# One more slot of P turned by DMA in the odd pairs, and the order of all steps taken from a table

## The chip, the cores and the metric

The kernel runs on one core of one Trainium2 chip. The time is the device time of one execution in microseconds (us). Before the change it is 818.27 us, the median of 3 runs (817.58 to 820.57).

## What is computed

The inputs are q, k and v with 8 batches, 12 heads, 448 rows and 64 columns, all float32. The reference, cut to what matters:

```python
q_n, k_n = rmsnorm(q, g_q), rmsnorm(k, g_k)
scores = q_n @ k_n.T / sqrt(64)
attn = exp(scores - max(scores));  attn = attn / (sum(attn) + 1e-9)
x = (attn @ v)                     # heads side by side: (8, 448, 768)
h = maximum(x @ w_in, 0.0)         # w_in: 768 x 1024
conv = sum(conv_w[i] * shifted(h, i - 1) for i in range(3))   # along the 448 rows
out = (h * sigmoid(conv)) @ w_out  # w_out: 1024 x 768
```

## The kernel before, in words

**The work and its tiles.** The 96 heads are taken two at a time: 48 pairs, n = 0 to 47, six to a batch. A pair's two 448 x 448 score matrices are cut into seven slots, each with 128 rows of P and 448 columns. For each pair the kernel loads q, k and v, squares and sums (`square`, `square_sum`, L384, L395), makes the reciprocal root in nine small steps (`rsqrt`, L416 to L431), applies it (`apply_rms`, the helper's L121, into the tile sq) and turns k and q (`qk_transpose`, L455). `v_bound` (L542) takes the largest v. `scores` (L633) puts two slots at a time into PSUM, `soft_max` takes the largest of a row on DVE, and `soft_exp` (L647) writes the exponentials of a slot to a tile e on ACT.

**Two ways for P.** The product with v (`pv`, L764) needs P turned, in the tile PT. From pair ten on the matrices go through TensorE as pairs of float16 numbers, a high and a low part, with three products for one. There a slot of P takes one of two ways:

- through TensorE: `p_transpose` (L677) turns the float32 exponentials in four blocks, `p_evac` (helper L109, ACT or DVE) copies them out of PSUM as the high part, and `p_low` (L693, DVE) subtracts to get the low part;
- through the DMA: `p_hi` (helper L109) writes the high part into one of four buffers ph, `p_lo` (helper L121) the low part, and `p_turn` (L669) issues a transposing DMA from the queue SP straight into PT.

`nd(n)` says how many slots go by DMA: none below pair ten, six of seven in even pairs, five in odd ones. Pairs below ten use float32 on TensorE and turn all seven slots there.

**The two products after it.** `x_scale`, `x_hi` and `x_lo` make x of a pair; `in_part` (L849) is three matmuls of the product with w_in, `in_relu` to `in_lo` make the gated h on ACT, DVE and POOL, and `out_part` (L918) is four or eight matmuls of the product with w_out. Matmuls of one batch are spread between the attention of the next one. At the start the two weights are loaded and split into float16 parts (`convert`, L228 to L236, `bound`, L286, `split`, `rest`, L313).

**What sets the order.** All of this is 4908 steps. A planner inside the kernel gives each step a due time (`PACE`, `SHIFT`, `base`), lists what it needs (`needs`) and which engines can take it at what cost (`options`), and then places step after step, always the one that its model could start first, weighed with the due time. The order so made is the order in which each engine, and the queue SP, runs its instructions; it fixes too which of two or three engines takes a step, and which PSUM bank. An engine never passes a waiting instruction.

Of the kernel before, what the change touches and what calls it, by code (L numbers as in the profile page):

```python
# [19 lines left out]
PH = dict(  # L20
    sh=10, sm=15, sw=0.0, f_pl=0.0375, f_ql=0.2981, f_lo=0.1439, f_rms=0.7618, f_sq=0.4266,
    T=17.3833, ti=41.4349, si=4.1104, so=8.3395, hop=0.86442, beta=0.01242, wi0=-50.4678,
    wi1=121.7101, wo0=25.8448, wo1=191.2771, cw=148.8611, p_evac=0.4491, p_hi=1.3981, p_lo=0.4268,
    p_rms=0.5211, p_v=0.5458, p_x=0.0, p_g=4.2741, p_relu=21.8931, p_cv=3.9149, p_ev=23.6856,
    sp=0.0518, nbulk=4, p_rs=0.0491, p_sq=1.6068, p_w=6.9093, v0=26.5245, nd=6, ng=5, cs=5, ct=3,
    cm=9, ne=5, n2=0, n1=10, q1=10, nf=10, pvs=4, p_sa=2.9086, p_c0=0.4899, p_ca=0.4662,
    p_ss=3.937, p_qh=2.0393, p_ql=2.1586, p_ph=3799.4719, p_pl=2744.2083, f_ca=0.232, f_cv=0.0,
    f_ev=0.0, f_evac=0.0, f_g=0.0, f_relu=0.0114, f_v=0.1905, f_w=0.0633, f_pl_early=0.0372,
    f_ql_early=0.301, f_lo_early=0.3185, f_rms_early=0.0046, f_sq_early=0.0131,
    p_evac_early=0.258, p_hi_early=0.2963, p_lo_early=0.4289, p_rms_early=0.4454,  # L30
    p_v_early=0.3813, p_x_early=0.7905, p_g_early=0.9472, p_relu_early=12.3484,
    p_cv_early=10.9077, p_ev_early=22.3546, p_rs_early=0.0395, p_sq_early=17.492,
    p_w_early=182.8497, p_sa_early=4.9153, p_c0_early=0.4104, p_ca_early=16.3838,
    p_ss_early=3.937, p_qh_early=3.8564, p_ql_early=3.3133, p_ph_early=10.4483,
    p_pl_early=23.3405, f_ca_early=0.5227, f_cv_early=0.2129, f_ev_early=0.0247, f_evac_early=0.0,
    f_g_early=0.0, f_relu_early=0.2356, f_v_early=0.0161, f_w_early=0.0241, early=9, f_sa=0.4067,
    f_sa_early=0.1734, f_x_early=0.0301, f_hi=0.1205, f_hi_early=0.0, f_x=0.0463, f_c0=0.0028,
    f_rs=0.0, f_rs_early=0.0121,
)
PACE = [  # L40
    19.5944, 19.8948, 16.4648, 19.6082, 13.2431, 14.9147, 11.825, 10.1937, 22.5592, 19.3385,
    25.6034, 15.2494,
]
SHIFT = dict(
    prepare=1144.827, load_g=408.072, make_g=1103.747, load_cw=607.34, make_cw=-40.693,
    load=31.489, convert=814.375, bound=1163.815, bound_max=1185.545, bound_turn=683.508,
    scale=1588.906, in_factor=1190.579, split=219.334, rest=-3.777, out_factor=13.562,
    load_k=276.969, load_q=-23.205, square=644.465, square_sum=176.751, rsqrt=204.636,
    apply_rms=466.723, qk_transpose=49.891, qk_hi=700.581, v_load=1413.524, v_bound=41.813,
    scores=154.339, soft_max=-4.033, soft_exp=1280.605, p_transpose=1204.209, p_evac=1.285,  # L50
    sum_add=984.669, sum_step=662.828, sum_store=217.691, sum_load=507.067, pv=524.491,
    x_scale=111.36, x_hi=969.665, x_lo=4.428, v_max=-17.121, v_turn=12.147, v_scale=833.202,
    qk_lo=-6.58, q_hi=-16.441, q_lo=262.726, q_turn=-4.581, p_hi=807.409, p_lo=-4.961,
    p_turn=606.498, p_low=0.411, v_hi=539.567, v_lo=817.516, moe_scales=2733.662,
    in_part=1631.107, in_relu=283.451, in_conv=494.692, in_tanh=706.753, in_gate=507.891,
    in_hi=1047.689, in_lo=2.125, in_carry=156.421, out_scales=760.141, out_part=104.873,
    out_evac=1.046, out_store=35.83, sum_spread=1.673, sum_turn=2.156,
)
SCHED = {}
ON_ACT = ""  # L60
# [20 lines left out]
def tile_attention_moe(ctx: ExitStack, tc, q, k, v, g_q, g_k, w_in, conv_w, w_out, out):  # L81
# [7 lines left out]
    P = 128  # L89
# [7 lines left out]
    T = PH["T"]  # L97

    def base(n):

        return sum(PACE[:n]) + max(n - len(PACE), 0) * T

    def queue(kind):
        return nc.scalar if kind in ON_ACT.split() else nc.sync

# [65 lines left out]
    def at(t, fn, *args):  # L171
        plan.append((t + SHIFT.get(fn.__name__, 0.0), len(plan), fn, args))
# [77 lines left out]
    def plan_weight(name, w, w32, s_col, free, t0, t1, after):  # L250
# [105 lines left out]
    def load_k(n):  # L356
        x = new("qkf", n, [PB, 2, 2, NB, D], F32)
        rows = slice(n * 2 * S, (n + 1) * 2 * S)
        queue("lk").dma_start(x[:, 1], heads(kf[rows].rearrange("(h p t) d -> p h t d", h=2, t=NB), n))

    def load_q(n):
# [147 lines left out]
    def plan_qk(n):  # L509
        s = base(n)  # L510
        at(s - 45.0, load_k, n)
        at(s - 45.0, load_q, n)
        for i in sides(n):
            at(s - 24.0, square, n, i)
            at(s - 22.0, square_sum, n, i)
            if duo(n)[0] == n:
                for j in range(NRS):
                    at(s - 20.0 + 0.3 * j, rsqrt, n, j, i)
        for i in (1, 0):
            at(s - 15.0 - i, apply_rms, n, i)  # L520
            if i == 0 and n >= PH["q1"]:
                at(s - 13.0, q_hi, n)
                at(s - 12.0, q_lo, n)
                at(s - 11.0, q_turn, n)
                continue
            at(s - 10.0 - i, qk_transpose, n, i)
            at(s - 8.0 - i, qk_hi, n, i)
            if not whole(n):
                at(s - 6.0 - i, qk_lo, n, i)


    def v_load(n):
        t = new("v", n, [PB, 2, NB, D], F32)
        rows = slice(n * 2 * S, (n + 1) * 2 * S)
        queue("lv").dma_start(t, vf[rows].rearrange("(h p t) d -> p h t d", h=2, t=NB))
# [24 lines left out]
    def plan_v(n):  # L560
        b, i = divmod(n, NP)
        t = base(max(n - 7, 0)) + PH["v0"] + 3.0 * min(n, 7)
        at(t, v_load, n)
        at(t + 20.0, v_bound, n)
        if i == NP - 1:
            at(t + 20.5, v_max, b)
            at(t + 20.6, v_turn, b)
            at(t + 22.0, v_scale, b)
# [31 lines left out]
    def nd(n):  # L600
        return 0 if n < PH["n1"] else (PH["nd"], PH["ne"], PH["nd"], PH["ng"])[n % 4]
# [108 lines left out]
    def sum_store(n):  # L710
        d = new("rd", n, [32, P], F32, pD)
        queue("rd").dma_start(d.rearrange("s (b i) -> b s i", b=4), old("rT", n))

    def shuffled(n):

        return n >= PH["sh"] and PH["sm"] >> n % 4 & 1
# [5 lines left out]
    def sum_load(n, h):  # L722
        d = old("rd", n)[:NS].rearrange("t p -> (t p)").rearrange("(h s) -> h s", h=2)
        if shuffled(n):
            r = fixed("row", n, rows).rearrange("(x p) s -> x p s", p=32)[:, 0]
            queue("rb").dma_start(r, d.unsqueeze(1).to_broadcast([2, 2, S]))
# [3 lines left out]
        queue("rb").dma_start(old("rB", n)[HALF[h]], d[h : h + 1].to_broadcast([64, S]))  # L730
# [59 lines left out]
    def plan_attention(n):  # L790
        s, d = base(n), (base(n + 1) - base(n)) / NS
        for g in groups(n):
            at(s + max(2 * g - n % 2, 0) * d, scores, n, g)
        for j in range(NS):
            at(s + j * d + 1.0, soft_max, n, j)
            at(s + j * d + 2.0, soft_exp, n, j)
            if j < nd(n):
                at(s + j * d + 3.0, p_hi, n, j)
                at(s + j * d + 4.0, p_lo, n, j)
                at(s + j * d + 5.0, p_turn, n, j)  # L800
                continue
            at(s + j * d + 4.0, p_transpose, n, j)
            at(s + j * d + 5.0, p_evac, n, j)
            if nd(n):
                at(s + j * d + 6.0, p_low, n, j)
        s += NS * d
        at(s + 2.0, sum_add, n)
        at(s + 2.5, sum_step, n)
        at(s + 3.0, sum_turn, n)
        at(s + 4.0, sum_store, n)  # L810
        for h in range(loads(n)):
            at(s + 6.0, sum_load, n, h)
        if shuffled(n):
            at(s + 7.0, sum_spread, n)
        if nd(n):
            at(s - 4.0, v_hi, n)
            at(s - 3.0, v_lo, n)
        for i, k in enumerate(pvs(n)):
            at(s + 8.0 + i, pv, n, k)
        at(s + 13.0, x_scale, n)  # L820
        at(s + 14.0, x_hi, n)
        at(s + 15.0, x_lo, n)
# [107 lines left out]
    def out_store(b, ch, half):  # L930
        row0 = out_place(b, ch)[1]
        queue("out").dma_start(
# [691 lines left out]
```

## Time and profile before

| what | before |
|---|---|
| median of 3 runs | 818.27 us |
| profiled execution, first to last instruction | 818.1 us |
| TensorE (PE) busy | 787.5 us, 96% |
| VectorE (DVE) busy | 704.5 us, 86% |
| ScalarE (ACT) busy | 683.4 us, 84% |
| GpSimd (POOL) busy | 445.9 us, 55% |
| DMA, share of 16 engines | 74.4% |

The profiled execution's span of 818.1 us is its own time here; no other time is given for it, and it lies 0.2 us below the median. Busy is the time in which at least one instruction of the engine runs. PE means matmuls, PEld loads of weights, SP the queue from which all DMAs are issued. A name like e_(25_5_5245 is the tile e of pair 25, slot place 5.

### The profile page before, as it was taken

To read this page: it belongs to the slowest core of one execution; us is meant where nothing else is said; L and a number is where in the kernel's file an instruction comes from. 1 tells how busy PE (TensorE), PEld (TensorE's weight loads), DVE (VectorE), ACT (ScalarE), POOL (GpSimd) and SP (SyncE) were. 2 spreads that over 40 slices of the span, in tenths; PEclk is the share of its full clock that TensorE was granted. 3 is DMA by queue.
4 is the path that set the end of the run, shared out by engine and by line. 5 is a ranking of instruction groups with operands and counts; after the bars stand their busy time and mean duration, and the time that the engine had idled before them with its cause. 6 is when DMAs were issued, how large, how long until landed. Compare 5 with 4: busy or idle time off the path is not lost.

```text
span 818.1 us, 16993 instructions
## 1 busy us (share of the span) xinstructions
PE 787.5 (96%) x5582; PEld 429.3 (52%) x5582; DVE 704.5 (86%) x1478; ACT 683.4 (84%) x1584; POOL 445.9 (55%) x575
## 2 busy tenths in 40 slices
PE   3889999999999999999999999999999999999998
PEld 1444555555555555555555565555555555555554
DVE  7999999999899989999899989999899988882420
ACT  4989999998899877998899887988899888981531
POOL 2222134585677656687578556686578566552220
PEclk9998999999999999999999999999999999999999
DMA  8765753369988999779998999889988997444001
GB/s 238 210 194 147 185 161 80 81 134 168 181 159 149 179 184 188 166 147 185 173 168 167 181 177 182 159 143 186 183 177 159 184 176 167 94 90 102 10 20 59
DMA packets 325453, 124.65 MB, mean 152 GB/s; under 512 B 270172, under 2 KB 321780, under 8 KB 325364
## 3 DMA queue, kind: packets, MB, share of 16 engines
q1 hardware_dynamic: 325364, 123.56, 74.4%
q8 instruction: 44, 0.72, 0.4%
q14 instruction: 45, 0.37, 0.2%
HBM read 48.20 MB, written 11.80 MB: 73 GB/s over the span
## 4 chain that ended last, share of the span: by engine, by line
PE 48%; DVE 13%; ACT 11%; DMA 6%; issue 4%; POOL 2%; SPq 2%; ACTq 0%; POOLq 0%; DVEq 0%
PE bank L918 21%; PE bank L849 11%; PE bank L764 6%; PE bank L633 6%; DMA PT<-ph 4%; PE bank L677 2%; ACT ph L109 2%; SPq L669 1%; PE bank L455 1%; POOL ph L121 1%; DMA rd<-rT 1%; DVE st L395 1%; DMA row<-rd 1%; DVE PT L693 1%; ACT bank L857 1%
## 5 line engine op out<-in xcount | busy, mean ns | idle before, releaser
L849 PE MATMUL bank<-x,wi 128*128 128x448 f16 x1152 | 231.7, 353 | 0.3 <-DVE PT L109 0.3
L918 PE MATMUL bank<-wo,gring 128*128 128x384 f16 (+1 forms) x1056 | 199.5, 327 | 1.0 <-ACT e_(34_4_7306 L647 0.8
L849 PEld LDWEIGHTS <-wi 128*128 128x128 f16 x1152 | 110.5, 98 | 103.9 <-issue 11.6
L918 PEld LDWEIGHTS <-gring 128*128 128x128 f16 (+1 forms) x1056 | 101.7, 99 | 67.9 <-issue 16.4
L633 PE MATMUL bank<-kT,qT 64*128 64x448 f16 (+3 forms) x1072 | 131.4, 392 | 1.3 <-ACT e_(3_2_713 L647 0.6
L764 PE MATMUL bank<-PT,vp 112*64 112x448 f16 x912 | 93.9, 354 | 1.4 <-ACT e_(27_0_5495 L647 1.0
L764 PEld LDWEIGHTS <-vp 112*64 112x64 f16 x912 | 50.5, 110 | 42.1 <-issue 15.0
L395 DVE TENSOR_REDUCE st<-sq 112x16 f32<-112x1024 f32 (+1 forms) x50 | 58.3, 1170 | 9.6 <-ACT sq L384 9.4
L633 PEld LDWEIGHTS <-qT 64*128 64x128 f16 (+1 forms) x912 | 33.2, 97 | 51.3 <-issue 31.6
L384 ACT ACTIVATE sq<-qkf 112x1024 f32<-112x1024 f32 (+1 forms) x48 | 49.6, 1033 | 5.2 <-DMA qkf<-in_q_dram 3.9
L121 POOL TENSOR_TENSOR sq<-qkf,st 112x512 f32<-112x512 f32 x38 | 39.9, 1056 | 19.1 <-issue 9.6
L121 POOL TENSOR_TENSOR x<-x,x 128x448 f16<-128x448 f32 x33 | 34.2, 1036 | 27.6 <-DVE x L109 12.3
L455 PE MATMUL bank<-ident,sq 112*128 112x112 f32 x232 | 33.0, 268 | 15.8 <-DVE G L974 10.3
L918 PE MATMUL bank<-wo,wi 128*128 128x384 f16 (+1 forms) x192 | 46.9, 326 | 0.0
L121 DVE TENSOR_TENSOR sq<-qkf,st 112x512 f32<-112x512 f32 x58 | 44.8, 791 | 0.1
L693 DVE TENSOR_TENSOR PT<-bank,PT 112x512 f16<-112x512 f32 x57 | 39.0, 684 | 3.2 <-ACT PT L109 2.8
L857 ACT ACTIVATE bank<-bank 128x448 f32<-128x448 f32 x64 | 34.4, 538 | 8.7 <-PE bank L849 7.9
L121 POOL TENSOR_TENSOR qkf<-sq,qkf 112x512 f16<-112x512 f32 x32 | 37.1, 1160 | 5.6 <-DVE sq L121 4.1
L455 PEld LDWEIGHTS bank<-ident,sq 112*128 112x128 f32 x232 | 25.8, 144 | 26.3 <-issue 14.6
L109 ACT COPY PT<-bank 112x512 f32<-112x512 f32 x62 | 36.2, 605 | 2.6 <-PE bank L677 2.3
L918 PE MATMUL bank<-wo,carry 128*64 128x384 f16 x192 | 34.0, 328 | 0.5 <-DVE c_(1_6_3169 L879 0.5
L542 DVE TENSOR_REDUCE vacc<-v 112x1 f32<-112x512 f32 x48 | 32.2, 674 | 2.4 <-DMA v<-in_v_dram 1.9
(2224 smaller groups left out, 1953.9 us busy)
## 6 DMA issues: line engine op xcount, KB each, us to landing
qkf<-in_k_dram SPq DMA_DIRECT2D x48, 224.0 KB
v<-in_v_dram SPq DMA_DIRECT2D x48, 224.0 KB
wo<-in_moe_w_in_dram SPq DMA_DIRECT2D x12, 512.0 KB
gring<-in_moe_w_out_dram SPq DMA_DIRECT2D x16, 384.0 KB
qkf<-in_q_dram SPq DMA_DIRECT2D x24, 224.0 KB
qkf<-in_q_dram SPq DMA_DIRECT2D x48, 112.0 KB
PT<-ph SPq DMA_TRANSPOSE x209
rB<-rd SPq DMA_DIRECT2D x20, 112.0 KB
```

The costliest lines, as they stand in the source:

```text
L109: (nc.scalar.copy if e == "ACT" else elementwise(e).tensor_copy)(dst, src)
L121: elementwise(e).tensor_tensor(dst, a, b, op=op)
L384: nc.scalar.activation(sq, x, AF.Square)
L395: nc.vector.tensor_reduce(st, sq, axis=AX.X, op=ALU.add)
L455: nc.tensor.transpose(ps[:, t * PB : (t + 1) * PB], x[:, t], ident[:PB, :PB])
L542: nc.vector.tensor_reduce(old("vacc", b)[:PB, i : i + 1], old("v", n).rearrange("p h t d -> p (h t d)"), axis=AX.X, op=ALU.max, apply_abso ...
L633: nc.tensor.matmul(ps[u][o, :S], lhs, rhs, start=(i == 0), stop=(whole(m) or i == 2),)
L693: nc.vector.tensor_tensor(turned(n, j, 1), held["t", ("p", n, j)][:PB].rearrange("p (k q) -> p k q", k=NB), turned(n, j, 0), op=ALU.subtract,)
L764: nc.tensor.matmul(ps[HALF[h], :S], lhs, rhs, start=(i == 0 and k == 0), stop=(i == pvs(n)[-1] and k == NB - 1),)
L849: nc.tensor.matmul(ps[:, :S], wi[:, wl, c, fc * P : (fc + 1) * P], old("x", b * NP + c)[:, xl], start=(i == 0), stop=(i == 3 * NP - 1),)
L857: nc.scalar.activation(ps, ps, AF.Relu, scale=2.0 ** -24)
L918: nc.tensor.matmul(ps[p0 : p0 + m, :NO2], g, wo[:, wl, fc, half * NO2 : (half + 1) * NO2], start=(i == 0), stop=(i == 3 * NFC - 1),)
```

## The change

`nd` becomes the list `ND`, with none for the first ten pairs and six for all others. So in the 19 odd pairs 11, 13, ... 47 slot place 5 leaves TensorE and goes by DMA: 19 `p_transpose`, 19 `p_evac` and 19 `p_low` go, 19 `p_hi`, `p_lo` and `p_turn` come. The planner with its due times and costs goes too. In its place stands a table of 4908 entries with the step, its engine and its PSUM banks; the steps are run in the table's order.

```diff
-    sp=0.0518, nbulk=4, p_rs=0.0491, p_sq=1.6068, p_w=6.9093, v0=26.5245, nd=6, ng=5, cs=5, ct=3,
-    cm=9, ne=5, n2=0, n1=10, q1=10, nf=10, pvs=4, p_sa=2.9086, p_c0=0.4899, p_ca=0.4662,
...
+ORDER = (
+    "$%&!!!#!$($!$)#!$*%!!*&!$+#!!.#!$&&!$q&!!+&!$,#!$-#!$.#!!/#!$3$!$s$!$/#!$0%!!#&!$r&!!,&!%a&!$4#!"
...
+ND = [0] * 10 + [6] * 38
...
     def nd(n):
-        return 0 if n < PH["n1"] else (PH["nd"], PH["ne"], PH["nd"], PH["ng"])[n % 4]
+        return ND[n] if 0 <= n < NPAIR else 0
...
-    while len(order) < len(steps):
-        best, free_banks = None, room()
...
+    for i in range(len(plan)):
+        a, b, e, z = (DIGITS.index(x) for x in ORDER[4 * i : 4 * i + 4])
+        fn, args = plan[len(DIGITS) * a + b]
+        step, e = (fn.__name__, *args), ("PE", "DVE", "ACT", "POOL", "SP")[e]
+        order.append((step, fn))
         on[step] = e
...
+        placed[step] = [y - 1 for y in divmod(z, 9) if y]
```

Nearly every step stands elsewhere than before. Steps that change engine, over the whole program: `apply_rms` from DVE to POOL (58 on DVE before, 12 now), `p_hi` (all 209 on ACT before; of 228 now 167 on ACT, 44 on POOL, 17 on DVE), `p_lo` (all 209 on POOL before; now 180, and 48 on DVE), `in_hi` (64 on ACT before; now 41, 17 on POOL, 6 on DVE), `in_lo` (64 on POOL before; now 50, 14 on DVE), `out_evac` (56 on ACT before; now 41, 15 on DVE), `p_evac` (33 on DVE before; now 9).

TensorE in pair 25, before: its slot place 5 is turned between two matmuls of the product with w_in (wi) and the scores of pair 26 (kT, qT).

```order
L849 LDWEIGHTS wi_84
L849 MATMUL bank_71<-x_4678,wi_84 128x448
L677 MATMUL bank_68<-ident,e_(25_5_5245 112x128 x4
L633 LDWEIGHTS qT_5058
L633 MATMUL bank_67<-kT_5070,qT_5058 128x448
```

The same place now: L1004 is `in_part`, L834 `p_transpose`.

```order
L1004 LDWEIGHTS wi_84
L1004 MATMUL bank_72<-x_4970,wi_84 128x448
L834 MATMUL bank_69<-ident,e_(25_6_5250 112x128 x4
L1004 LDWEIGHTS wi_84
L1004 MATMUL bank_73<-x_4755,wi_84 128x448
```

Place 5 is gone from TensorE; place 6 alone is turned there, between matmuls of the product with w_in.

ACT at the same pair, before: after the exponentials of places 5 and 6 it copies place 5 out of PSUM (PT from a bank).

```order
L647 ACTIVATE e_(25_5_5245,rsum_82<-bank_67,sst_(25_5_5232 128x448
L647 ACTIVATE e_(25_6_5262,rsum_82<-bank_66,sst_(25_6_5247 128x448
L109 CAST PT_5171<-bank_68 112x4x128
L109 CAST ph_79<-e_(25_3_5179 128x4x112
L109 CAST ph_80<-e_(25_4_5191 128x4x112
L109 CAST PT_5171<-bank_66 112x4x128
```

ACT now: L804 is `soft_exp`, L270 the copying helper.

```order
L804 ACTIVATE e_(25_6_5250,rsum_82<-bank_69,sst_(25_6_5226 128x448
L270 CAST ph_78<-e_(25_3_5182 128x4x112
L270 CAST ph_79<-e_(25_4_5199 128x4x112
L270 CAST ph_80<-e_(25_5_5216 128x4x112
L804 ACTIVATE e_(26_0_5271,rsum_81<-bank_67,sst_(26_0_5258 128x448
```

The copy of place 5 out of PSUM has become a third write into a buffer ph, behind which a low part and a DMA follow.

DVE at the start of the program, before, in pair 1's softmax: it applies the root to q of pair 2 (sq from qkf) between the largest v (vacc) of two pairs and a copy of P.

```order
L416 SCALAR_TENSOR_TENSOR st_228<-st_228 112x32
L542 TENSOR_REDUCE vacc_288<-v_291 112x1
L109 COPY PT_386<-bank_68 112x4x128
L121 TENSOR_TENSOR sq_229<-qkf_165,st_228 112x2x4x64
L639 TENSOR_REDUCE sst_(1_5_420<-bank_72 128x1
L542 TENSOR_REDUCE vacc_288<-v_332 112x1
```

POOL now, at that place: L282 is the helper of `apply_rms`, L577 to L590 are steps of `rsqrt`.

```order
L590 TENSOR_TENSOR st_254<-st_254 112x32
L588 TENSOR_TENSOR st_254<-st_254 112x32
L577 TENSOR_SCALAR st_254<-st_254 112x32
L578 TENSOR_TENSOR st_254<-st_254 112x32
L282 TENSOR_TENSOR sq_255<-qkf_138,st_254 112x2x4x64 x2
L857 TENSOR_SCALAR rsum_82<-rsum_82 128x7
```

Both applications of pair 2, q and k, stand on POOL now; one of them stood on DVE.

## Rows read from the trace of the kernel before

**Rows 1.** The page's first part: busy time and share of each engine.

```profile
PE 787.5 (96%) x5582; PEld 429.3 (52%) x5582; DVE 704.5 (86%) x1478; ACT 683.4 (84%) x1584; POOL 445.9 (55%) x575
```

**Rows 2.** By stretch: length; busy PE, PEld, DVE, ACT, POOL; granted clock; DMA; GB/s.

```profile
0.00:117.00 117.00, 96.19 (x543) 52.11 (x543) 109.45 (x264) 101.58 (x243) 32.18 (x72) 0.97 0.69 188
60.00:80.00 20.00, 17.91 (x87) 10.17 (x88) 19.81 (x48) 18.85 (x42) 5.04 (x12) 0.83 0.49 134
117.00:186.50 69.50, 68.26 (x420) 35.79 (x419) 66.72 (x142) 66.81 (x154) 39.51 (x45) 1.00 0.47 109
186.50:818.10 631.60, 623.03 (x4623) 341.38 (x4622) 528.37 (x1073) 515.05 (x1190) 374.22 (x459) 1.00 0.79 151
```

**Rows 3.** Engines that PE waited for, late and early: us in total, times, longest.

```profile
PE bank L455 <- DVE G L974: 10.3, 1, 10.3
...
PE bank L677 <- ACT e_(25_5_5245 L647: 0.7, 1, 0.7
...
PE bank L677 <- ACT e_(37_5_7912 L647: 0.4, 1, 0.4
PE bank L764 <- DMA PT<-ph: 0.4, 1, 0.4
```

**Rows 4.** The chain that ended last, pieces on PE: start us, us, what, matmuls.

```profile
275.00 0.44 PE bank L677 x4
...
277.33 0.76 PE bank L918 x4
...
278.53 1.30 PE bank L918 x8
...
755.57 27.24 PE bank L849 x144
```

**Rows 5.** Writers of ph and PT by tile: duration ns least/median/most, first and last start.

```profile
L669 SPq DMA_TRANSPOSE PT<-ph x209: 1231/1262/2733, 159.9 to 744.1; - x105
...
L121 POOL TENSOR_TENSOR ph<-e_(10_1_1782,ph x1: 1047/1047/1047, 158.2 to 158.2; 128x448 f16<-128x448 f32 x1
```

**Rows 6.** DVE, groups by line and shape: busy us, mean ns of one, idle before.

```profile
L121 DVE TENSOR_TENSOR sq<-qkf,st 112x512 f32<-112x512 f32 x58 | 44.8, 791 | 0.1
...
L542 DVE TENSOR_REDUCE vacc<-v 112x1 f32<-112x512 f32 x48 | 32.2, 674 | 2.4 <-DMA v<-in_v_dram 1.9
...
L313 DVE SCALAR_TENSOR_TENSOR wi<-wi,wsc 128x1024 f16<-128x1024 f32 x6 | 7.6, 1274 | 0.0
...
L109 DVE COPY PT<-bank 112x512 f32<-112x512 f32 x8 | 5.4, 679 | 0.9 <-ACT e_(8_1_1383 L647 0.5 <-PE bank L677 0.3
...
L424 DVE TENSOR_SCALAR st<-st 112x32 int32<-112x32 int32 x23 | 3.9, 170 | 0.2
L700 DVE TENSOR_SCALAR rsum<-rsum 128x7 f32<-128x7 f32 x12 | 3.6, 299 | 0.0
```

**Rows 7.** ACT, groups by line and shape, the same columns.

```profile
L109 ACT COPY PT<-bank 112x512 f32<-112x512 f32 x62 | 36.2, 605 | 2.6 <-PE bank L677 2.3
...
L109 ACT CAST x<-x 128x448 f16<-128x448 f32 x31 | 17.8, 574 | 6.1 <-DVE x L775 5.6 <-DVE x L778 0.4
...
L286 ACT ACTIVATE wo<-wo 128x384 f16<-128x384 f32 x16 | 8.8, 549 | 0.2
```

**Rows 8.** Time line of the end: the last store, issued from SP.

```profile
815.16 0.33 SPq L932 DMA_DIRECT2D out_dram<-c_('o'_7_3_1_10763  x1
```

**Rows 9.** DVE instructions with two inputs in SBUF: ns least/median/most.

```profile
L121 DVE TENSOR_TENSOR sq<-qkf,st x58: 636/682/1531, 9.5 to 685.8; 112x512 f32<-112x512 f32 x58
...
L121 DVE TENSOR_TENSOR x<-x,x x15: 582/615/985, 138.0 to 727.1; 128x448 f16<-128x448 f32 x15
```

**Rows 10.** Time line around P times v of pair 18, SP and PE.

```profile
301.40 2.73 SPq L669 DMA_TRANSPOSE PT<-ph  x2
...
307.37 2.43 PE L764 MATMUL bank<-PT,vp 112*64 112x448 f16 x23 [0.37 <-DMA PT<-ph]
```

**Rows 11.** ACT's wait for a free buffer ph: us in total, times, longest.

```profile
ACT ph L109 <- DMA PT<-ph: 26.4, 34, 2.6
```

More of the change, by code (lines that the diff above doesn't have):

```diff
@@ L40 @@
[L40 to L58, printed above, removed]
@@ L931, in out_store @@
         row0 = out_place(b, ch)[1]
[L932 removed]
+        nc.sync.dma_start(
             outf[row0 : row0 + P, half * NO2 : (half + 1) * NO2],
@@ L1357, in tile_attention_moe @@
-    PATIENCE = dict(
-        qk_hi="hi", q_hi="qh", q_lo="ql", apply_rms="rms", x_hi="x", x_lo="lo", in_hi="g", in_lo="g",
-        out_evac="ev", sum_add="sa", v_hi="hi", v_lo="lo", p_hi="ph", p_lo="pl", v_bound="v", rest="w", rsqrt="rs", square="sq", convert="c0", in_relu="relu", in_conv="cv", p_evac="evac", in_carry="ca",
-    )
-    def takes(name, *a):
-        if name in ("qk_transpose", "p_transpose", "bound_turn", "v_turn"):
-            return "t", (give(name, *a),)
-        if name in ("in_part", "out_part") and not a[-2] or name == "pv" and not a[-1]:
-            return "m", (give(name, *a),)
-        if name == "scores":
-            return "s", tuple(("soft_exp", *x) for x in members(*a))
-        if name == "in_conv" and not a[-1] or name == "out_evac":
-            return "c", (give(name, *a),)
-        return None
@@ L1387, in tile_attention_moe @@
-    steps = {(fn.__name__, *args): (t, i, fn) for t, i, fn, args in plan}
-    assert len(steps) == len(plan)
-    after, left, ready, done = {}, {}, {}, {}
-    for step in steps:
-        pre = {p for p in needs(*step) if p in steps}
-        left[step], ready[step] = len(pre), []
-        for p in pre:
-            after.setdefault(p, []).append(step)
-    waiting = {e: {} for e in ("PE", "DVE", "ACT", "POOL", "SP")}
-    MOE = ("in_", "out_", "moe_")
-    def patience(i, name, *a):
-        kind = ("p_" if i else "f_") + PATIENCE.get(name, "")
-        if a and isinstance(a[0], int) and a[0] < (1 if name.startswith(MOE) else PH["early"]):
-            kind += "_early"
-        return kind
@@ L1406, in enqueue @@
-    def enqueue(step):
-        for i, (e, c, dma) in enumerate(options(*step)):
-            t = max((end + lat["DMA" if dma else e] for end, lat in ready[step]), default=0.0)
-            waiting[e][step] = t + PH.get(patience(i, *step), 0.0), c, dma
-    sys.setrecursionlimit(20000)
-    due = {}
-    def urgency(step):
-        if step not in due:
-            due[step] = min(
-                [steps[step][0]] + [urgency(p) - PH["hop"] for p in after.get(step, ())]
-            )
-        return due[step]
@@ L1433, in tile_attention_moe @@
-    WINDOW = 4096 / 1200
-    free = dict.fromkeys(waiting, 0.0)
-    pmode, port = None, dict(DVE=0.0, POOL=0.0)
-    turn, held_by = None, {}
-    def mode(name, *a):
-        if name == "scores" and a[0] % 2 and not a[1]:
-            return "middle"
-        return name if name in ("pv", "scores") else ""
-    ringq = {"m": [], "c": [], "t": [], "s": []}
-    most = dict(s=PH["cs"], t=PH["ct"], m=PH["cm"], c=BUFS["c"])
-    last_in, placed = [None] * NBANK, {}
-    def back_at(step, e, dma):
-        if step is None:
-            return 0.0
-        if step not in done:
-            return None
-        x = engine[step]
-        return done[step] + LAT["DMA" if x[2] else x[0]]["DMA" if dma else e]
@@ L1574, in tile_attention_moe @@
-    SCHED.update(held_by=held_by, after=after, t=max(done.values()), t0=0.0, done=done, engine=engine, order=order)
+    order, placed, held_by, turn = [], {}, {}, None
+    for i in range(len(plan)):
[3 more added lines that the diff above has]
+        order.append((step, fn))
+        on[step] = e
+        placed[step] = [y - 1 for y in divmod(z, 9) if y]
+        if shared(e, step[0]):
+            if e == "DVE":
+                turn = step
+            elif turn:
+                held_by[step], turn = turn, None
@@ L1582, in tile_attention_moe @@
     with tc.manual_schedule():
-        for step in order:
-            taken[:] = placed.get(step, ())
+        for step, fn in order:
+            taken[:] = placed[step]
             start = len(nc.cur_bb.bb.instructions)
-            steps[step][2](*step[1:])
+            fn(*step[1:])
             if step in owners:
```

867 lines of the change are left out of this document (295 added, 572 removed).

## The prediction

> **What bounds the kernel now.** I read the busy shares first: matmuls run in 96% of the span, VectorE in 86%, ScalarE in 84%, GpSimd in 55% [rows 1]. Such shares are averages, so the second view is the busy time by stretch [rows 2]. It shows two regimes. From 117 us on, TensorE is busy in 68.3 of 69.5 us and then in 623.0 of 631.6 us: it alone sets the end there, and a microsecond less of matmul work is a microsecond less of span, as long as the others keep up. Before 117 us it is busy for 96.2 us only, while VectorE has 109.5 and ScalarE 101.6: there TensorE waits for what these two make. Third, the waits of TensorE [rows 3]: one of 10.3 us at the start, and after it nothing long; a turned P that came by DMA was waited for once, 0.4 us. Fourth, the pieces of the chain that lie on TensorE [rows 4], for the price of its work: 144 matmuls of the product with w_in take 27.24 us, 0.19 us each; eight of the product with w_out take 1.30 us, but four that stand alone after scores take 0.76 instead of 0.65, so a change between kinds of work costs about 0.11 us.
>
> **The parts, and what each costs.**
>
> *19 transposes leave TensorE.* Four blocks of one slot take 0.44 us [rows 4]; 19 x 0.44 = 8.3 us. From pair eleven on TensorE is the bound [rows 2], so all of it counts: -8.3. The Trainium skill speaks against this move (VectorE: DVE Perf Modes, The three transpose paths, and the rules behind it): it wants a 128 x 128 block turned on TensorE where PSUM will do, 390 ns against 1309 ns by DMA. If the longer way were paid by who waits, 19 x 0.92 us would be added, 17.5 us, and the time would be 836 us (an estimate from that page). The trace agrees that the DMA way is longer, 1262 ns for the issue alone [rows 5], but not that TensorE pays it [rows 3].
>
> *Waits in front of those transposes.* Two of them stand among the waits: 0.7 us for the exponential of pair 25 and 0.4 us for pair 37 [rows 3]. The instruction that waited is gone; the matmuls behind it don't need that slot. -1.1; it is 0 if the neighbour that now comes first waits as long.
>
> *Copies and low parts.* On VectorE and ScalarE 19 `p_evac` and 19 `p_low` go, and 19 `p_hi` and `p_lo` come; from 186.5 us on VectorE is busy 528 and ScalarE 515 of 632 us [rows 2], so either sign is hidden. Its cover is gone only if one of them comes near the whole stretch. GpSimd has 374 of 632 us there; it gives up 48 `p_lo` to VectorE and 14 `in_lo`, at 1.05 us each [rows 5], and takes 46 `apply_rms`, 44 `p_hi` and 17 `in_hi`. That leaves it some 50 us fuller by my count, still under 70%.
>
> *19 DMA transposes more.* Each holds SP for 1.26 us [rows 5], 24 us over 600. The 209 of before were waited for 0.4 us by TensorE [rows 3]. I take 0; the bounds are 0 and rival C.
>
> *The start.* By the order, the steps placed before the first scores of pair 8 (117 us in the trace) change so. VectorE loses three `apply_rms` (44.8/58 = 0.77 us), two `v_bound` (0.67), two `p_evac` (0.68), one `rest` (1.27) and seven small instructions at 0.17, and takes five `sum_add` of 0.30 [rows 6]: -2.3 - 1.3 - 1.4 - 1.3 - 1.2 + 1.5 = -6.0 us. ScalarE loses three `x_hi` at 0.57 and two `bound` at 0.55 and takes one `p_evac` at 0.58 (36.2/62) [rows 7]: -2.2 us. Both were close to full, so that point should come between 2.2 and 6.0 us earlier; I take the middle, 4.1. TensorE meanwhile has three `in_part` more (3 x 3 x 0.19 = 1.7 us) and two transposes of four blocks fewer (2 x 0.44), so 0.8 us of its later work is already done. Together -4.9; the bounds are 0 (the wait moves to a place I have not counted, the 10.3 us at the start stay in any case) and -6.8.
>
> *Changes of kind.* I counted in both orders how often TensorE goes from scores, P times v or the rest to another of the three: 264 before, 273 now. 9 x 0.11 = +1.0 us; the bounds are 0 and twice that.
>
> *The clock.* In the stretch from 60 to 80 us the granted clock is 0.83 on average [rows 2], so TensorE was at the lower of its levels (1.2 of 2.4 GHz) for a third of it; 0.17 x 20 = 3.4 us of full-speed time. It had been waiting on and off before. The new order keeps a start of the same kind, so I leave the dip: 0, with bounds of -3.4 (gone) and +3.4 (a second one).
>
> *The rest of the order.* Nearly every step has moved. From 117 us on TensorE is idle for 1.2 + 8.6 = 9.8 us [rows 2]; of that the last store, issued at 815.2 us, and the copy before it take some 4 us after the last matmul [rows 8], which stay, and 1.1 are counted. What is left, about 4.7, may go or double: 0, bounds -4.7 and +4.7.
>
> **Sum.** Against the profiled execution's 818.1 us: -8.3 - 1.1 - 4.9 + 1.0 = -13.3, that is 804.8. The median of the runs is 0.2 above the span of the profile, so **805 us**.
>
> **Rivals.**
>
> *A: the order gains more.* The start comes to its far bound (-1.9 more), the dip of the clock goes (-3.4) and the later idle time too (-4.7): 795. For it: the wait behind each of these is named above. Against it: three things must go well at once.
>
> *B: VectorE and GpSimd block each other.* Two inputs from SBUF make an instruction on VectorE run late beside GpSimd: `apply_rms` has a median of 682 ns but a longest of 1531, `x_lo` 615 and 985 [rows 9]. By the Trainium skill (SBUF — State Buffer, Who interferes with whom) such a pair excludes each other for a whole instruction; the rows agree for their slowest, whose excess of 0.85 us is no more than one GpSimd instruction of 1.05. 48 `p_lo` and 14 `in_lo` of this kind come to VectorE and 46 `apply_rms` leave it. If each of the 62 stood for half a GpSimd instruction, 0.52 us, VectorE would have 32 us more. It has 103 us free after 186.5 us [rows 2], most of it in the last 80; if a third of the 32 us falls where a matmul waits, 11 us are lost: **816**, no change. Against it: the mean of `apply_rms` lies only 0.09 us over its median (0.77 and 0.68), and that makes 62 x 0.09 = 5.6.
>
> *C: the turned P comes late, slower than before.* The way over TensorE from the exponential to a ready slot is 0.44 + 0.60 + 0.68, 1.7 us (the low part priced as the copy of the same shape) [rows 4, 6, 7]. By DMA it is about 0.57 for the high part, 1.05 for the low one, 1.26 for the issue [rows 5, 7], and then until the data is there: for pair 18 the second issue ended at 304.13 and P times v went on at 307.37 [rows 10], 3.2 us. That is 6.1, 4.4 longer. Now 61 of the high parts are written by GpSimd or VectorE, and they wait for a free buffer ph as ScalarE did, 34 times for 26.4 us [rows 11]; GpSimd's low parts, behind them in its queue, would hold up the next DMA. If P times v of each odd pair came 1.5 us late, 19 x 1.5 = 28.5 us would turn 805 into **833**. It decides where the cover runs out. Counted in TensorE's order with the prices above, between the scores of place 5 and P times v of an odd pair lie 12.4 us of matmuls at least and 18 in the middle; even pairs, which sent that place by DMA before, had 17.1 at least. So only the tight ones (three of 19 are under 14 us) are near it, and the chain of 6.1 us would have to double. Nearly no wait for it in the trace [rows 3] speaks against it too.
>
> *D: the change does less.* Transposes fall away, but the start stays as it is: 818.1 - 8.3 - 1.1 + 1.0 + 0.2 = 810. If the waits in the middle then double too, 815.
>
> **The numbers.** A measurement of this kernel can tell a change of about 0.5%, 4.1 us, from none; faster means under 814.2, slower over 822.4. Chances: the forecast, 799 to 810, 0.58; A, below 799, 0.14; D within the gain, 810 to 814, 0.10; B and the end of D, no change, 0.10; C, slower, 0.08. So faster 0.82, same 0.10, slower 0.08. The range has to leave out no more than 0.2: I cut A's far end at 796 and reach to B's lower part at 815, which leaves out about 0.05 below and 0.15 above.
>
> **What would show it.** Matmuls busy for about 776 us in a span of 805; 108 groups of `p_transpose` in place of 127; 228 DMA transposes into PT; the first scores of pair 8 at 113 us, with VectorE and ScalarE still near full before. The wait of P times v for its DMA stays under 2 us in all. Wrong would be: `pv` among the waits of TensorE with more than 10 us (C); VectorE's `p_lo` with a mean far over 0.68 us and TensorE waiting for VectorE after 186 us (B); or pair 8 at 117 us again (D).

## The result, and the profile after

The changed kernel takes 811.6 us, the median of 4 runs (810.8 to 813.6), where the kernel before takes 818.5 beside it. The ratio is 0.9915, with a 95% interval of 0.9892 to 0.9938: 6.9 us less, about half of the 13.3 us that were forecast. A second time, beside other kernels (below), it was 0.9924 [0.9908, 0.9941], 6.2 us less.

The page's first part for the kernel after, which answers to [rows 1]:

```profile
PE 778.7 (96%) x5506; PEld 416.7 (52%) x5506; DVE 703.8 (87%) x1507; ACT 635.4 (79%) x1485; POOL 492.4 (61%) x634
```

There are 76 matmuls fewer, 19 x 4, and TensorE is busy 8.8 us less. GpSimd is 46.5 us fuller, ScalarE 48 us emptier. The same view by stretch as [rows 2], with the last stretch to the new end (length; busy PE, PEld, DVE, ACT, POOL; granted clock; DMA; GB/s):

```profile
0.00:117.00 117.00, 98.09 (x569) 52.13 (x570) 109.32 (x268) 103.16 (x248) 37.74 (x74) 1.00 0.70 186
60.00:80.00 20.00, 19.45 (x107) 9.21 (x106) 19.89 (x46) 19.73 (x46) 6.66 (x13) 1.00 0.53 144
117.00:186.50 69.50, 69.21 (x448) 36.80 (x447) 66.39 (x140) 67.55 (x160) 46.27 (x55) 1.00 0.57 131
186.50:809.00 622.50, 611.43 (x4493) 327.75 (x4491) 528.09 (x1100) 464.73 (x1079) 408.39 (x505) 1.00 0.83 159
```

Two things are to be seen. The half-speed stretch of before between 60 and 80 us (0.83) is not there in this execution. And from 186.5 us on TensorE is idle for 11.1 us, where it was 8.6 in [rows 2]: although it has less to do, it waits more. Its waits after the start are short and go mostly to exponentials of ScalarE (waits of PE; us in total, times, longest):

```profile
PE bank L614 <- DVE sq L282: 10.6, 1, 10.6
...
PE bank L834 <- ACT e_(15_6_3000 L804: 1.5, 1, 1.5
...
PE bank L834 <- ACT e_(19_6_3924 L804: 0.5, 1, 0.5
...
PE bank L1004 <- ACT e_(27_1_5502 L804: 0.5, 1, 0.5
```

The exponentials of pairs 25 and 37 that [rows 3] showed are gone, and others stand in their place; the DMA into PT is not among the waits. ScalarE, GpSimd and VectorE wait for a free buffer ph (waits of these three, as [rows 11]):

```profile
ACT ph L270 <- DMA PT<-ph: 22.4, 23, 6.0
...
POOL ph L270 <- DMA PT<-ph: 7.5, 4, 3.4
...
DVE ph L270 <- DMA PT<-ph: 1.7, 1, 1.7
```

Together 31.6 us, more than the 26.4 before. These are the lines on which the experiments turn. Last, the DMA transposes (duration ns least/median/most) and the first scores of pair eight on the time line of PE:

```profile
L826 SPq DMA_TRANSPOSE PT<-ph x228: 1231/1258/3013, 153.6 to 735.6; - x114
```

```profile
113.19 1.02 PE L790 MATMUL bank<-kT,qT 64*128 64x448 f32 x4
```

228 of them as foreseen, and pair eight at 113.2 us where 113 was forecast.

For the experiments I priced every step of TensorE at what the quickest tenth of its kind takes in the trace of before, from its start to that of the next step (a slot's transposes 0.436 us, three matmuls with w_in 0.567, four with w_out 0.650, P times v 0.756, scores 0.578). The sum is the **work**; what a trace has over it, stalls and half speed together, is the **loss**.

### The profile page after: what moved, and what is told of

The parts are those of the page before. It is cut to its first block, busy times and chain, and to the rows that moved or that the text cites. A ratio compares the mean times of both kernels' runs of the same rounds, so it can differ in the third digit from the quotient of the medians.

```text
span 809.0 us, 16810 instructions
## 1 busy us (share of the span) xinstructions
PE 778.7 (96%) x5506; PEld 416.7 (52%) x5506; DVE 703.8 (87%) x1507; ACT 635.4 (79%) x1485; POOL 492.4 (61%) x634
## 4 chain that ended last, share of the span: by engine, by line
PE 45%; DMA 7%; DVE 7%; ACT 5%; POOL 4%; issue 3%; SPq 1%; POOLq 0%; ACTq 0%; DVEq 0%
PE bank L1073 18%; PE bank L1004 14%; PE bank L921 6%; DMA PT<-ph 6%; PE bank L790 5%; POOL ph L282 2%; PE bank L834 1%; DMA qkf<-in_q_dram 1%; PE bank L614 1%; POOL sq L282 1%; DVE x L932 1%; ACT ph L270 1%; DVE vacc L700 0%; DMA row<-rd 0%; DVE PT L850 0%
## 5 line engine op out<-in xcount | busy, mean ns | idle before, releaser
L1004 PE MATMUL bank<-x,wi 128*128 128x448 f16 x1152 | 230.8, 353 | 2.1 <-DVE x L932 0.7
L1004 PEld LDWEIGHTS <-wi 128*128 128x128 f16 x1152 | 110.0, 98 | 108.0 <-issue 14.7
L790 PE MATMUL bank<-kT,qT 64*128 64x448 f16 (+3 forms) x1072 | 133.5, 391 | 3.6 <-DVE x L932 0.7
L282 POOL TENSOR_TENSOR sq<-qkf,st 112x512 f32<-112x512 f32 x84 | 88.0, 1056 | 40.1 <-DVE wo L393 7.6
L282 POOL TENSOR_TENSOR x<-x,x 128x448 f16<-128x448 f32 x37 | 38.4, 1037 | 18.7 <-DVE wo L397 7.7
L1012 ACT ACTIVATE bank<-bank 128x448 f32<-128x448 f32 x59 | 31.7, 540 | 22.0 <-PE bank L1004 22.0
L282 POOL TENSOR_TENSOR qkf<-sq,qkf 112x512 f16<-112x512 f32 x35 | 41.3, 1181 | 7.4 <-DVE ph L282 1.6
L270 ACT COPY PT<-bank 112x512 f32<-112x512 f32 x66 | 38.1, 600 | 1.4 <-PE bank L834 1.4
L1073 PE MATMUL bank<-wo,carry 128*64 128x384 f16 x192 | 35.3, 329 | 0.0
L921 PE MATMUL bank<-PT,v 112*64 112x448 f32 x160 | 32.3, 545 | 0.2 <-ACT PT L270 0.2
L1073 PE MATMUL bank<-wo 128*128 128x384 f16 (+1 forms) x96 | 31.3, 326 | 0.0
```

Of the source, the lines that this page charges most:

```text
L270: (nc.scalar.copy if e == "ACT" else elementwise(e).tensor_copy)(dst, src)
L282: elementwise(e).tensor_tensor(dst, a, b, op=op)
L790: nc.tensor.matmul(ps[u][o, :S], lhs, rhs, start=(i == 0), stop=(whole(m) or i == 2),)
L921: nc.tensor.matmul(ps[HALF[h], :S], lhs, rhs, start=(i == 0 and k == 0), stop=(i == pvs(n)[-1] and k == NB - 1),)
L1004: nc.tensor.matmul(ps[:, :S], wi[:, wl, c, fc * P : (fc + 1) * P], old("x", b * NP + c)[:, xl], start=(i == 0), stop=(i == 3 * NP - 1),)
L1012: nc.scalar.activation(ps, ps, AF.Relu, scale=2.0 ** -24)
```

## The experiments

The theory at the start: TensorE sets the time, so the slot move gives back its 8.3 us and the order only the start. The rivals: the order is what gains; P comes late; part of a saving on TensorE turns into waits. "Six" below is a kernel with six buffers ph in place of four. The runs came in three groups, each on a chip of its own; all ratios are to before in the same group, which had medians of 820.9, 820.9 and 820.0 us, and a comparison across groups goes by these ratios; 0.001 is 0.8 us.

| order of the steps | slots of odd pairs by DMA | four ph | six ph |
|---|---|---|---|
| before | five | 1 | 0.9975 [0.9961, 0.9989] |
| before, slot five put in | six | 1.0824 [1.0799, 1.0848] | 1.0256 [1.0237, 1.0274] |
| the planner's, made anew | six | 1.0222 [1.0198, 1.0246] | 1.0017 [1.0001, 1.0032] |
| new | five | 0.9935 [0.9915, 0.9955] | 0.9931 [0.9908, 0.9954] |
| new | six | 0.9924 [0.9908, 0.9941] | 0.9854 [0.9836, 0.9872] |

### The slot move alone

The order of before, written as a table, with six slots in the odd pairs: 19 `p_transpose`, `p_evac` and `p_low` taken out, `p_hi` on ACT where the copy stood (or behind the high part of slot four), `p_lo` on POOL and `p_turn` on SP right behind those of slot four.

```diff
-        return 0 if n < PH["n1"] else (PH["nd"], PH["ne"], PH["nd"], PH["ng"])[n % 4]
+        return ND[n] if 0 <= n < NPAIR else 0
+ND = [0] * 10 + [6] * 38
```

> The order of the kernel before, with the slot move alone: in the 19 odd pairs from 11 on, the transposes, their copy and low part of slot five go, and a high part on ScalarE, a low part on GpSimd and a DMA transpose stand in their places. Theory 1 (TensorE sets the time, each of the 19 tiles that it no longer turns gives back 0.44 us, and the new order is worth little): 8.3 us under before, about 810, and TensorE's work down by 8.3 us. Rival 2 (the gain of the change is in its new order): within 2 us of before, about 818. Rival 3 (P comes late by DMA where the order was not made for it): slower than before, 822 or more, with waits of the P V matmuls for the DMA transposes.

Measured: 888.3 us, 1.0824. The slot move by itself loses 67 us. The work fell by the 8.3 us as reckoned; the loss after pair ten rose from 33.6 to 110.5 us. Some 16 us of this rise is the clock: after its stalls (last section) TensorE ran for 32 us at the lower of its two levels, and in before for none after 150 us. Rival 3 had the sign, but not the place: P times v waits for its DMA once, 0.7 us. The waits of ACT and PE in this kernel:

```profile
ACT ph L270 <- DMA PT<-ph: 87.2, 53, 4.7
```

```profile
PE bank L834 <- ACT e_(30_6_6339 L804: 7.9, 1, 7.9
PE bank L834 <- ACT e_(42_6_8988 L804: 7.4, 1, 7.4
PE bank L834 <- ACT e_(36_6_7676 L804: 3.6, 1, 3.6
```

How the two hang together stands on the time line of ACT at pairs 29 and 30 (start, us, what; in brackets idle before and what ended it):

```profile
492.32 0.56 ACT L270 CAST ph<-e_(29_3_6066 128x448 f16<-128x448 f32 x1
492.77 0.57 ACT L270 CAST ph<-e_(29_4_6101 128x448 f16<-128x448 f32 x1
496.73 0.56 ACT L270 CAST ph<-e_(29_5_6114 128x448 f16<-128x448 f32 x1 [3.38 <-DMA PT<-ph]
...
505.77 0.56 ACT L270 CAST ph<-e_(30_1_6210 128x448 f16<-128x448 f32 x1 [3.17 <-DMA PT<-ph]
...
512.18 0.56 ACT L270 CAST ph<-e_(30_2_6234 128x448 f16<-128x448 f32 x1 [4.74 <-DMA PT<-ph]
...
513.88 0.64 ACT L804 ACTIVATE e_(30_6_6339<-bank,sst_(30_6_6322 128x448 f32<-128x448 f32 x1
```

The high part of slot five of pair 29 waits 3.4 us for a buffer, the next ones 3.2 and 4.7; the exponential of place six of pair 30 stands behind all of them on ScalarE and starts at 513.88; and TensorE, which is to turn that place next, waits:

```profile
514.66 1.10 PE L834 MATMUL bank<-ident,e_(30_6_6339 128*112 128x128 f32 x4 [7.87 <-ACT e_(30_6_6339 L804]
```

A buffer is held long: 30_2 is the fourth write after 29_4, so it takes that buffer again, 512.18 - 492.77 = 19.4 us later. In between the low part on GpSimd, the place in SP's queue and the DMA itself have to pass. GpSimd (two low parts) and SP on the time line:

```profile
494.21 1.03 POOL L282 TENSOR_TENSOR ph<-e_(29_4_6101,ph 128x448 f16<-128x448 f32 x1
...
506.42 1.03 POOL L282 TENSOR_TENSOR ph<-e_(30_1_6210,ph 128x448 f16<-128x448 f32 x1 [2.56 <-ACT ph L270]
```

```profile
507.48 4.01 SPq L826 DMA_TRANSPOSE PT<-ph  x3
```

The low part of 29_4 ends at 495.2, but in the kernel's table its DMA stands behind that of 30_1, and the low part of 30_1 had to wait for the very high part that waited. The three DMAs are those of 30_1, 29_4 and 29_5: 29_4's starts at 508.8, so 13.5 of the 19.4 us are its wait in SP's queue. In the table place 4 stands behind place 1 of the next pair in two odd pairs only, 29 and 41, and the two longest stalls above follow on these, in pairs 30 and 42; in the order of after place 4 stands so in no pair, place 5 in three. Before has the same order at these places, but with five slots. So it is too few buffers together with the place at which they are given back; no run moved these DMAs alone, so what the place is worth by itself is not shown.

### The slot move with the planner's order

```diff
-    sp=0.0518, nbulk=4, p_rs=0.0491, p_sq=1.6068, p_w=6.9093, v0=26.5245, nd=6, ng=5, cs=5, ct=3,
-    cm=9, ne=5, n2=0, n1=10, q1=10, nf=10, pvs=4, p_sa=2.9086, p_c0=0.4899, p_ca=0.4662,
+    sp=0.0518, nbulk=4, p_rs=0.0491, p_sq=1.6068, p_w=6.9093, v0=26.5245, nd=6, ng=6, cs=5, ct=3,
+    cm=9, ne=6, n2=0, n1=10, q1=10, nf=10, pvs=4, p_sa=2.9086, p_c0=0.4899, p_ca=0.4662,
```

> The kernel before with its planner told to give six slots of every pair from ten on to the DMA, so the slot move with an order that the planner makes anew. Theory 1: about 810, as the slot move alone, give or take 4 us for the planner's other order. Rival 2 (the table's order is what gains): 816 to 822. If this is well above the slot move alone, a new plan by itself costs several us, and the order of a plan is a term as large as the slot's.

Measured: 839.0 us, 1.0222. So the loss is not a fault of my placing alone: the planner, which counts the buffers among what a step needs, still loses 18 us. Neither theory 1 nor rival 2 had this. ScalarE waits 36.4 us for ph here, 43 times.

### The order alone

The new order with slot five of the odd pairs given back to TensorE, as the expectation says; in the table 57 entries change their step, and banks from pair eleven on.

```diff
-ND = [0] * 10 + [6] * 38
+ND = [0] * 10 + [6, 5] * 19
```

> The new order with slot five of the odd pairs given back to TensorE: 19 transposes, copies and low parts put in where the trace of after has room, and the banks dealt anew from there on (waits for a bank of up to 3.6 us in all, counted from that trace). Theory 1: 8.3 us over after for the work and 0 to 4 us for the banks, 820 to 824. Rival 2 (the order holds the gain): 812 to 815.

Measured: 815.7 us, 0.9935. Rival 2 is right on the size, 0.7 us above its range: the order gives 5.3 us by itself, and the slot move within it, 0.9935 to 0.9924, only 0.9 us, give or take 2.1, which can't be told from nothing. TensorE waits three times for a low part of VectorE in this trace, 2.3 us in all, and never in that of after; if this comes from my placing of the 19 steps, the slot move is worth still less. Its waits for ph are well below those of after (ACT and POOL):

```profile
ACT ph L270 <- DMA PT<-ph: 10.5, 11, 2.8
...
POOL ph L270 <- DMA PT<-ph: 7.4, 3, 5.0
```

### The price of TensorE's work, and after once more

```diff
-        for kt in range(NB):
+        for kt in list(range(NB)) * (2 if nd(n) and n % 2 else 1):
```

> After, with the four transposes of slot six issued twice into the same bank in the 19 odd pairs: TensorE gets back 19 tiles of 0.436 us, and nothing else changes. Theory 1: 8.3 us over after, 820 (7 to 9 us). Rival 4 (the stalls of TensorE after 140 us, some 12.8 us of them, would take in a part of the work, since a later wait ends at the same time): 2 to 5 us over after, 814 to 817, and the stalls shorter by the difference.

> The changed kernel itself beside the others of this call, so that differences of 2 to 5 us are read against it on the same chip. Every theory: 0.989 to 0.994 of before.

Measured: 818.4 us, 0.9968 [0.9953, 0.9982], against 0.9924 for after: 3.6 us more, give or take 1.8, for 8.3 us of matmuls. (The two stand in different groups, each against before in its own.) Rival 4 holds. TensorE is busy for 96% of the time and yet only a part of a change in its work comes out as time, 1.8 to 5.4 of 8.3 us: the loss after pair ten is 36.4 us here and 38.6 and 40.8 in the two traces of after.

### Six buffers

New theory: with four buffers ph, the chain high part, low part, DMA runs the buffers out, ScalarE waits, and the exponentials behind it come late. Six buffers, with 9 of x in place of 12 for the room, in the slot move alone, in after, in the order alone, in before (its order word for word), and with the planner.

```diff
-        qkf=3, sq=2, st=2, qT=2, kT=2, v=8, sst=6, e=4, PT=2, x=12, c=3,
-        rB=2, x32=1, vacc=2, vsc=4, cwb=3, rd=2, rsum=2, rT=1, row=1, ph=4, vp=2,
+        qkf=3, sq=2, st=2, qT=2, kT=2, v=8, sst=6, e=4, PT=2, x=9, c=3,
+        rB=2, x32=1, vacc=2, vsc=4, cwb=3, rd=2, rsum=2, rT=1, row=1, ph=6, vp=2,
```

> The slot move alone in the order of before, which took 888 us, with six buffers for the halves of P in place of four (their room comes from the tile x, 9 buffers in place of 12); order and engines are the same. Theory 5 (the fifth low part per odd pair makes ScalarE wait for a free buffer of the halves, 87.2 us in 53 waits, and the next exp, on which TensorE's transpose of slot six hangs, stands behind that wait): those waits of ScalarE fall below 30 us, TensorE's waits for exp of slot six (8.0 us the longest) go, and the time falls to 810 to 822. Rival 6 (the buffers are not it: ScalarE has too much to do, or the DMA transposes stand too late in SP's queue): over 860, with TensorE waiting for the same steps.

> The changed kernel with six buffers for the halves of P in place of four, and 9 of x in place of 12. Theory 5: the 22.4 us that ScalarE waits for a buffer of the halves fall below 8, and the part of TensorE's stalls after 140 us that comes from them (about 4 of 12.8 us) goes: 2 to 6 us under after, 806 to 810 where after has 812. Rival 7 (what is left of those waits is hidden): within 1 us of after.

> Order alone (the new order with slot five of the odd pairs on TensorE, 815.7 us, ScalarE waiting 10.5 us for buffers of the halves) with six such buffers and 9 of x. Beside the changed kernel with six buffers (808.5) this gives the price of the slot move where buffers don't hold it. Theory 5 (a tile moved off TensorE is worth its 0.44 us, 8.3 us in all, and the four buffers took most of that back): within 2 us of order alone, 814 to 816, so 5.5 to 8 us over the changed kernel with six. Rival 10 (the buffers gain the same with five slots as with six, and the moved slot is worth little in any case): 6 us under order alone, about 810, within 2 us of the changed kernel with six.

> The kernel before, its order word for word, with six buffers for the halves of P in place of four and 9 of x in place of 12. Theory 5 (buffers matter where six slots load them; with five, ScalarE's 26.4 us of waits in before stand mostly beside TensorE's work): those waits fall below 8 us and the time falls by 0 to 4 us. Rival 11 (the buffers alone are the gain, with or without the change): 6 us or more under before, 815 or less where before has 820.9.

> The planner of before told to give six slots of every pair to the DMA (839.0 us) with six buffers for the halves and 9 of x, so an order that the planner makes with these buffers known to it. Theory 5: ScalarE's 36.4 us of waits for buffers go and it comes to 815 to 825. Rival 12 (its order is late for other reasons): over 830.

Measured: 842.1, 808.5, 814.7, 817.9 and 821.8 us; the ratios stand in the table. In after the waits for ph shrink to one line, of POOL:

```profile
POOL ph L270 <- DMA PT<-ph: 2.1, 1, 2.1
```

What follows, from the last two rows of the table: with four buffers the slot move is worth 0.0011, with six 0.0077 (6.3 us, give or take 2.4), and six buffers are worth 5.7 us with six slots, 0.3 with five. The two differences differ by 5.4 us, give or take 3.2. So it is the slot move that uses the buffers up, and they took most of its gain. Before gains 2.1 us of six, so buffers alone are not the change. What 9 of x in place of 12 costs by itself was not tried; in the order alone both together change nothing (0.9935 and 0.9931). The loss of TensorE by kernel (us, from the traces):

| kernel | work | loss to the scores of pair ten | loss after | waits for ph, all engines |
|---|---|---|---|---|
| before | 738.8 | 30.9 | 33.6 | 26.4 |
| order alone | 738.8 | 25.9 | 34.4 | 18.6 |
| after | 730.5 | 25.1 | 38.6 | 31.6 |
| after, again | 730.5 | 26.0 | 40.8 | 34.2 |
| after, six | 730.5 | 25.9 | 35.3 | 2.1 |
| order alone, six | 738.8 | 25.4 | 31.4 | none |
| slot move alone | 730.5 | 31.4 | 110.5 | 87.2 |
| slot move alone, six | 730.5 | 31.8 | 61.5 | 4.9 |

The expectation of the slot move alone with six missed: its waits for ph went and 46 us with them, but 21 us over before stayed. ScalarE carries all 228 high parts there, while after has given 61 of them to GpSimd and VectorE; that this is the rest was not tried, nor were the DMAs moved in SP's queue, so it stays open. The planner with six comes to no change, 1.0017: its time is what theory 5 said, but not by its way, since only half of ScalarE's waits went (36.4 to 19.0 us):

```profile
ACT ph L109 <- DMA PT<-ph: 19.0, 26, 2.6
```

Even with the buffers there, the table's order is worth 13 us over it; what in the order brings this was not tried.

After with six buffers beats both kernels: 808.5 us, 0.9854.

### The start alone

The new order up to the first scores of pair ten, then that of before, with five slots.

```diff
-ND = [0] * 10 + [6] * 38
+ND = [0] * 10 + [6, 5] * 19
```

> The new order up to the first scores of pair ten (143.3 us there, 149.3 in the trace of before, of which the half-speed stretch of that execution took 3.4), and the order of before from there, with five slots in the odd pairs as before. Theory 1 (start worth 2.6 us, or up to 6.0 if the half-speed stretch belongs to the old order): 2.6 to 6.0 us under before, 814.9 to 818.2 where before has 820.8. Rival 8 (the waits of the start are made up for later): within 1 us of before. Rival 9 (the start is the whole of what order alone gave): the same as order alone, 5 us under before, or lower.

Measured: 819.6 us, 0.9985 [0.9970, 1.0001]. The kernel so joined gains 1.3 us, give or take as much, between theory and rival 8. By this, of the 5.3 us of the order alone about 4 come after pair ten. But the join costs something itself: right behind it TensorE waits for two exponentials of pair nine, which it does neither in before nor in after (waits of PE from 140 to 156 us):

```profile
PE bank L834 <- ACT e_(9_6_1736 L804: 1.2, 1, 1.2
PE bank L614 <- ACT e_(9_5_1721 L804: 0.5, 1, 0.5
```

Without these 1.7 us the start would be worth up to some 3, and the rest of the order about 2; the runs don't settle the split.

### Steps moved at stalls

After with six buffers, and one group of scores of each of seven pairs (13, 14, 21, 23, 33, 39, 44) put behind one or two ready steps in TensorE's order. The first of them in the table:

```diff
-    "-x#!-r&!0s#!/3#!Kg!!0]&!-F#!/8#!/9$!KX&!-v%!-w&!-}#!-y$!-~$!,_#!/|%!.L!M/:%!/;&!.M!@Kn!!-D#!-z$!"
-    ".!$!-{%!-|&!Kh!!.%#!Jg$!/4%!.&$!1Y#!1Z#!Ko!!1[!#.+#!->#!.P#!.,$!Kp!!Ki#!Kj&!.($!1L&!/5!+.Q$!.-!&"
+    "-x#!-r&!0s#!/3#!Kg!!0]&!-F#!/8#!/9$!KX&!-v%!-w&!-}#!-y$!-~$!,_#!/|%!.L!M/:%!/;&!Kn!!Kh!!-D#!-z$!"
+    ".!$!-{%!-|&!.M!@.%#!Jg$!/4%!.&$!1Y#!1Z#!Ko!!1[!#.+#!->#!.P#!.,$!Kp!!Ki#!Kj&!.($!1L&!/5!+.Q$!.-!&"
```

There `.M!@` is the second scores of pair 13; `Kn!!` and `Kh!!`, two steps of the product with w_out, now stand before it.

> The changed kernel with six buffers, and seven steps of TensorE in whose front it stalled (0.4 to 1.1 us each, 5.3 us in all by the trace of that kernel) put behind one or two steps that were ready: scores 13, 14, 21, 33, 39 and 44, each one group later. If a stall is lost for good, 2 to 5 us under the changed kernel with six buffers, 803 to 807. If a step moved later only moves the wait to the softmax and the transposes behind it: within 1 us of it, or slower.

Measured: 808.5 us, 0.9851 [0.9827, 0.9875], the same as without (0.9854). The loss after pair ten is 35.4 us for 35.3: the stalls have moved and not gone. (The expectation's list leaves out pair 23, which was moved too.)

## Why the prediction came out as it did

The sign and the range held, and TensorE's records did what was foreseen: busy 778.7 us for about 776, 228 DMA transposes, pair eight at 113 us, P times v hardly waiting. The time gained is about half of the forecast. That 811.6 lies between 796 and 815 is luck in part: the rest of the order, counted as 0, gave up to 4 us, and the slot move and the start alone, as measured, would have come to about 816. By its own steps:

- *19 transposes leave TensorE, -8.3.* The work fell by 8.3 us in every trace. In time it is 0.9 us with four buffers, give or take 2.1. The sentence that failed is "it alone sets the end there, and a microsecond less of matmul work is a microsecond less of span, as long as the others keep up": they did not.
- *19 DMA transposes more, 0.* This is the term where the gain went. I priced the transposes by whether P times v waits for them, 0.4 us in [rows 3], and that stayed so. Their price was paid elsewhere: a buffer ph that is not free, ScalarE at a standstill, exponentials late, TensorE waiting for these. The row for it, [rows 11], I had, and used only in rival C, whose point of decision (the matmuls between the scores of place five and P times v) is not the one that decided. With four buffers the term is 7.4 us (8.3 - 0.9); with six it is 2.0, give or take 2.4, and the move gives 6.3 us.
- *Waits in front of pairs 25 and 37, -1.1.* They went, and waits of the same kind came for other pairs: 0, the other end that I had named.
- *The start, -4.9.* The point came where forecast. The half-speed stretch between 60 and 80 us, which the trace of before has and that of after has not (the loss there is 7.9 and 4.2 us), can't be counted as gain: of the 57 runs of before in the three groups the four at a granted clock of 1.000 took 820.7 us on average and the 28 at 0.996 or less 821.0. Measured by itself the start gives 1.3 us, up to 3 without the waits at the join. I had taken the work that two engines lose there for time, and it was so for a quarter of it, at most for some 60%.
- *The rest of the order, 0 with bounds of 4.7 either way.* About -4.1 (0.9985 to 0.9935), or -2 if the waits at the join are taken off, within its bounds. Part of it shows in the waits for ph: 18.6 us in the order alone, 29.7 in the start alone, which has the order of before from pair ten on, both with five slots.
- *The clock, 0.* The half-speed stretch comes and goes from one execution to the next, with either order. It is rarer in the new one: 17 of the 43 runs wholly in the new order have a mean granted clock of 0.999 or more, and 5 of the 69 of before with four and six buffers. In the times of before it does not show (the start, above); whether it does in the new order stays open.
- *What lies around the span, 0.2.* The time of the profiled execution of after is 810.79 us and its span 809.0: 1.8 us, not 0.2. I had set a span against a median of other runs. With 1.8 the forecast would have been 806.6.
- *Changes of kind, +1.0.* Not tried apart.

The terms as measured, -0.9 - 1.3 - 4.1, make -6.3, which is after's 0.9924; they are steps from one kernel to the next, so they have to.

Of the rivals, B did not come: the 48 low parts on VectorE have a median of 0.62 and a mean of 0.70 us, 3.8 us over the median in all, and no long wait of TensorE for VectorE stands after 186 us. D's 810 to 815 is where the time came out, by another way than D said. C was the mechanism nearest to what happened: in the old order the slot move is slower by more than its 833, and the new order is what keeps it away.

The Trainium skill (VectorE: DVE Perf Modes, Rules for kernel authors) wants such a tile turned on TensorE where PSUM will do. The runs agree in the old order (67 us lost) and differ in the new one with six buffers (6.3 us gained): what decides here is whether the buffers of the longer way last, not which way takes longer. (The 836 us that I worked out from that page took its two durations once for a slot, which is four blocks.) The Trainium skill (Perfetto Trace Analysis, Optimization Strategy) says that the same gap again and again on the engine that should be full can mean too few buffers. Here the gaps that show it were on ScalarE, 53 of them in the slot move alone, and not first on TensorE.

## What to carry to other kernels

Before work is moved off a full engine onto a longer way, count the buffers of that way: how long one is held (here up to 19 us), where in which queue it is given back (here 13.5 of the 19 us), and which engine stands still when none is free; and follow that engine's queue to what the full engine waits for next. A wait for a transfer that the consumer does not show can still be paid by the producer. And a busy share of 96% does not mean that a microsecond of work is a microsecond of time: give the engine known extra work and measure what comes out (here 3.6 of 8.3 us, give or take 1.8).

## What was not expected of the hardware

In the slot move alone TensorE's clock falls in or after its long stalls. Around the one at 506 us (length; busy PE, PEld, DVE, ACT, POOL; granted clock; DMA; GB/s):

```profile
490.00:506.00 16.00, 16.00 (x131) 8.58 (x126) 10.29 (x22) 8.67 (x21) 6.81 (x11) 1.00 0.85 162
506.00:514.00 8.00, 0.79 (x5) 0.27 (x3) 5.47 (x14) 3.26 (x10) 2.95 (x6) 0.88 0.65 136
514.00:519.00 5.00, 4.34 (x20) 2.73 (x22) 2.25 (x4) 4.43 (x10) 4.08 (x5) 0.51 0.79 174
519.00:530.00 11.00, 11.00 (x88) 6.03 (x83) 8.72 (x20) 9.68 (x23) 5.88 (x6) 1.00 0.76 133
```

TensorE stood still from 506.8 to 514.7 us. The granted clock fell while it stood (0.88 in that row), and up to 519 us it was 0.51, the lower of its two levels (1.2 of 2.4 GHz); then full speed again. The 4.3 us of matmuls at the lower level did about 2.2 us of full-speed work, so a stall of 7.9 us cost about 10. By the granted clock in this trace, after 150 us TensorE was busy for 32 us at the lower level, which is 16 us of work lost, out of 77 us by which its loss rose.

The mean granted clock also differs between executions of one kernel. In the start alone it goes from 0.995 to 1.000; the two runs at 1.000 took 816.0 and 817.7 us and the ten others 817.8 to 822.1. In before there is no such difference in time: its runs at 1.000 took 819.9 to 821.5 us.
